# Second-half decay exponentials made between the two halves of kernel generation, and four 64-column products of a transform in a row

## The chip, the cores and the metric

The kernel runs on one core of a Trainium2 chip. The metric is the time of one execution on the device in microseconds (us).

The engines are called as in the profile: PE is the TensorE (PEld its weight loads), DVE the VectorE, ACT the ScalarE, POOL the GpSimd, SP the queue that issues most DMAs.

## The reference, cut to what matters

The reference computes a forward and a backward pass of `x + S4(layernorm(x)) + FFN(layernorm(x))`, length 2048, width 576. The gated FFN has 4608 hidden columns. The S4 layer builds a convolution kernel of length 2048 from 128 modes per channel and applies it by Fourier transforms:

```python
P = jnp.exp(logdA[:, :, None] * l[None, None, :])          # decay exponentials
K = jnp.einsum("dn,dnl,dn->dl", Cc, P, dB).real            # kernel generation
Kf, Uf = rfft2(pad(K)), rfft2(pad(u))
y = irfft2(Uf * Kf)[:L] + u * Dskip
...
_out, _vjp = jax.vjp(_f, ...); return (_out, *_vjp(grad_out))
```

## The kernel before: the parts that matter

Two streams of Python generators are woven into one program. The FFN stream handles 12 chunks of 384 hidden columns. Each chunk starts with the weight gradients of the chunk before (16 to 48 products into one PSUM buffer for each evacuation). Then follow units with a DVE or ACT evacuation after every 3 to 6 products. The S4 stream has these passes: `p1(0)`, `p1(1)` (transform of the inputs, one for each half of the channels), `p2(0)`, `p2(1)` (kernel generation, then `param_grads`), and `p3(0)`, `p3(1)` (transform of the kernel). What a generator yields is its **plan**: microseconds that it takes in the estimate. The weaving uses plan time alone:

```python
PACE = 0.9
W1, W2, W3 = 60.0, 400.0, 58.0
...
    for us in ffn.gen(ln, final):                          # main loop
        ft += us
        ...
        while s4_open and stt < PACE * (ft - start):
            stt += next(sgen)                              # S4 stream (cut)

    def gen(self):                                         # the S4 stream (cut)
        yield from self.both(self.p1(0, 4, 10.0), 68.0, self.params(pw), 45.0)
        ...
        yield from self.both(self.p2(0, pools, pw), 0.8 * W2, self.p1(1, 2, 3.0), W1)
        yield from self.both(self.p2(1, pools, pw), 0.8 * W2, self.p3(0, 2, 3.0), W3)
        yield from self.p3(1, 4, 8.0)
```

A scheduler then orders the instructions of each engine anew; program order is its priority, not the final order. (In the trace of before, the first DVE operation of `p2(1)` starts at 899.99 us, ahead of the last one of `p2(0)`, at 901.46 us.) Each engine then works through its list in order.

The exponentials stand in `params`, two 16-channel groups in each step, for later use through DRAM. The mix is a transform step with 64 output columns for each product; its two outputs take one PSUM buffer each, of three that the S4 stream has:

```python
            def ex_step(i):                                # in params
                shp = [P, 2 * SX, NE]
                ex = exp_.tile(shp, F32, name="exs")       # pool of 3
                v.tensor_tensor(ex[:], pw[...], self.ev[...], op=ALU.mult)
                nc.scalar.activation(ex[:], ex[:], ACT.Exp)
                nc.sync.dma_start(self.ex_dram[:, i:i + 2], ex[...])
            for i in range(0, 8, 2):
                ex_step(i)
                yield 2.0
            ...                                            # other parameters
            for i in range(8, D // SX, 2):
                ex_step(i)
                yield 2.0

    def mix(self, dst, src):
        for o in range(2):
            ps = self.ps()
            for i in range(2):
                nc.tensor.matmul(ps[i * 64:(i + 1) * 64, :DH], lhsT=self.FM[:, o, :], rhs=src[:, i, :], ...)
            g.bal.copy(dst[:, o, :], ps[:, :DH], DH)
            if o == 0:
                yield 0.15
```

Of the kernel before, what the change touches and what calls it, by code (L numbers as in the profile page):

```python
# [2 lines left out]

# [456 lines left out]
class S4:  # L460
# [84 lines left out]
    def params(self, pw):  # L545
        g, nc, bal = self.g, self.g.nc, self.g.bal
        v = nc.vector
        with ExitStack() as c:
            pool = self.pool(c, "par_raw", 1)
            exp_ = self.pool(c, "par_ex", 3)  # L550
            raw = pool.tile([P, 6, D], BF16, name="raw")
            nc.sync.dma_start(raw[:], self.par_in[:])
            ldt = pool.tile([P, D], BF16, name="ldt")
            nc.sync.dma_start(ldt[:], self.log_dt.rearrange("(o d) -> o d", o=1).to_broadcast([P, D]))
            yield 1.0
            dt = pool.tile([P, D], F32, name="dtf")
            nc.scalar.activation(dt[:], ldt[:], ACT.Exp)
            nc.sync.dma_start(self.dt_dram[:], dt[:])
            Ar, Ai, Br, Bi, Cr, Ci = (raw[:, i, :] for i in range(6))
            v.tensor_tensor(pw[:, 0, :], Ar, dt[:], op=ALU.mult)  # L560
            bal.add(d=0.7, a=0.7)
            yield 1.0

            def ex_step(i):
                shp = [P, 2 * SX, NE]
                ex = exp_.tile(shp, F32, name="exs")
                v.tensor_tensor(ex[:], pw[:, 0, i * SX:(i + 2) * SX].unsqueeze(2).to_broadcast(shp), self.ev[:].unsqueeze(1).to_broadcast(shp), op=ALU.mult)
                nc.scalar.activation(ex[:], ex[:], ACT.Exp)
                nc.sync.dma_start(self.ex_dram[:, i:i + 2], ex[:].rearrange("p (i d) e -> p i d e", d=SX))
                bal.add(d=1.4, a=1.2)  # L570

            for i in range(0, 8, 2):
                ex_step(i)
                yield 2.0
            p1 = pool.tile([P, D], F32, name="p1")
            p2 = pool.tile([P, D], F32, name="p2")
            v.scalar_tensor_tensor(pw[:, 1, :], Ai, 1.0 / TWO_PI, dt[:], op0=ALU.mult, op1=ALU.mult)
            for j, (y1, y2, op) in enumerate(((Br, Bi, ALU.subtract), (Bi, Br, ALU.add))):
                v.tensor_tensor(p1[:], Cr, y1, op=ALU.mult)
                v.tensor_tensor(p2[:], Ci, y2, op=ALU.mult)  # L580
                v.tensor_tensor(p1[:], p1[:], p2[:], op=op)
                v.tensor_tensor(pw[:, 2 + j, :], p1[:], dt[:], op=ALU.mult)
                bal.add(d=2.6)
                yield 2.0
            for i in range(8, D // SX, 2):
                ex_step(i)
                yield 2.0

    def dft(self, pool, dram):
        def load(m):  # L590
# [26 lines left out]

    def mix(self, dst, src):
        g, nc = self.g, self.g.nc
        for o in range(2):  # L620
            ps = self.ps()
            for i in range(2):
                nc.tensor.matmul(ps[i * 64:(i + 1) * 64, :DH], lhsT=self.FM[:, o, :], rhs=src[:, i, :], start=True, stop=True)
            g.bal.copy(dst[:, o, :], ps[:, :DH], DH)
            if o == 0:
                yield 0.15

    def unmix(self, dst, src):
        g, nc = self.g, self.g.nc
# [33 lines left out]
    def p1(self, hf, n, gap):  # L663
        g, nc = self.g, self.g.nc
        cols = slice(hf * DH, (hf + 1) * DH)
        with ExitStack() as c:
            ap = self.pool(c, f"p1_a{hf}", n, "right")

            def load(m):
                t = ap.tile([P, 2, 2, DH], BF16, name="sig")  # L670
                nc.sync.dma_start(t[:, 0], g.xn_dram[:, 2 * m:2 * m + 2, cols])
                nc.sync.dma_start(t[:, 1], g.g_v[:, 2 * m:2 * m + 2, cols])
                return lambda i, n2: t[:, i, n2 % 2, :]
            yield from self.fwd1(hf, 2, load, ap, n, gap)
        with ExitStack() as c:
            bp = self.pool(c, f"p1_b{hf}", n, "right")
            fp = self.pool(c, f"p1_f{hf}", 2, "right")
            pp = self.pool(c, f"p1_p{hf}", 1, "right")

            def load_b(h):  # L680
                b = bp.tile([P, 2, 2, DH], BF16, name="b_ug")
                nc.sync.dma_start(b[:], self.mix_in(self.A[2][hf], h))
                return b
            bs = Ahead(load_b, ST, n)
            Z = None
            for h in range(ST + 1):
                old, Z = Z, None
                if h < ST:
                    b = bs.get(h)
                    if h == 0:  # L690
                        yield gap
                    sg = fp.tile([P, 2, 2, DH], BF16, name="s_ug")
                    for i in range(2):
                        yield from self.mix(sg[:, i], b[:, :, i, :])
                        yield 0.15
                    nc.sync.dma_start(self.S[hf][h], sg[:])
                    Z = self.product(fp, pp, sg[:, 1], sg[:, 0], True)
                    yield 0.7
                if old is not None:
                    Ct = fp.tile([P, 2, 1, DH], BF16, name="fC1")  # L700
                    yield from self.unmix(Ct[:, :, 0, :], old)
                    nc.sync.dma_start(self.mix_in(self.C[1][hf], h - 1), Ct[:])
                    yield 0.5
        with ExitStack() as c:
            bp = self.pool(c, f"p1_c{hf}", n + 1, "right")
            dp = self.pool(c, f"p1_d{hf}", 2, "right")

            def load_c(n2):
                Ct = bp.tile([P, 2, 1, DH], BF16, name="bC1")
                nc.sync.dma_start(Ct[:], self.C[1][hf][:, n2])  # L710
                return Ct
            Sx, cs = Ahead(self.dft(bp, self.s3_dram), ST // 2, n), Ahead(load_c, ST, n + 1)
            for n2 in range(ST):
                if n2 % 2 == 0:
                    S3 = Sx.get(n2 // 2)
                Ct = cs.get(n2)
                if n2 == 0:
                    yield gap
                if n2 % 4 == 0:
                    dk = dp.tile([P, DH // SC, 4, SC], BF16, name="dk")  # L720
                g.bal.copy(dk[:, :, n2 % 4, :], self.back2(S3[:, n2 % 2], Ct, 0).rearrange("p (g d) -> p g d", d=SC), DH)
                if n2 % 4 == 3:
                    nc.sync.dma_start(self.dk_dram[hf][:, n2 // 4], dk[:])
                yield 0.5

    def p3(self, hf, n, gap):
# [13 lines left out]
        with ExitStack() as c:  # L740
            bp = self.pool(c, f"p3_b{hf}", n, "right")
            fp = self.pool(c, f"p3_f{hf}", 2, "right")
            zp = self.pool(c, f"p3_z{hf}", 3, "right")
            pp = self.pool(c, f"p3_p{hf}", 1, "right")

            def load_b(h):
                b = bp.tile([P, 2, 1, DH], BF16, name="b_k")
                nc.sync.dma_start(b[:], self.mix_in(self.A[1][hf], h))
                sg = bp.tile([P, 2, 2, DH], BF16, name="s_ug")
                nc.sync.dma_start(sg[:], self.S[hf][h])  # L750
                return b, sg
            bs = Ahead(load_b, ST, n)
            Z = None
            for h in range(ST + 1):
                old, Z = Z, None
                if h < ST:
                    b, sg = bs.get(h)
                    if h == 0:
                        yield gap
                    sk = fp.tile([P, 2, DH], BF16, name="s_k")  # L760
                    yield from self.mix(sk[:], b[:, :, 0, :])
                    Z = self.product(zp, pp, sg[:, 0], sk[:], False), self.product(zp, pp, sg[:, 1], sk[:], True)
                    yield 0.7
                if old is not None:
                    for i in range(2):
                        Ct = fp.tile([P, 2, 1, DH], BF16, name="fC2")
                        yield from self.unmix(Ct[:, :, 0, :], old[i])
                        nc.sync.dma_start(self.mix_in(self.C[2][hf], h - 1)[:, :, i:i + 1, :], Ct[:])
                        yield 0.5
# [207 lines left out]
    def gen(self):  # L977
# [4 lines left out]
        with ExitStack() as cp:  # L982
# [9 lines left out]
            with ExitStack() as c:  # L992
                pools = self.p2_pools(c)
                yield from self.both(self.p2(0, pools, pw), 0.8 * W2, self.p1(1, 2, 3.0), W1)
                yield from self.both(self.p2(1, pools, pw), 0.8 * W2, self.p3(0, 2, 3.0), W3)
            yield from self.p3(1, 4, 8.0)

class Final:
# [201 lines left out]
```

## Time and profile before

| | before |
|---|---|
| time, median of 6 runs | 1849.15 us (1847.29 to 1854.74) |
| PE, DVE, ACT busy | 94%, 75%, 63% |
| exponentials | 18 double steps at 101 to 201 us |
| products of the mix | 384, in 141 groups without a full-width product between them |

The page of the kernel before: busy time, then the span in 40 slices (busy tenths of PE, and the clock that the throttle granted, in tenths).

```profile
PE 1732.4 (94%) x16110; PEld 1180.8 (64%) x16257; DVE 1378.4 (75%) x3223; ACT 1173.4 (63%) x2647; POOL 206.0 (11%) x246
...
PE   7989989999999999999999999999999998899888
...
PEclk9989999999999999999999999999999999999999
```

The windows view of before: stretch, its length, busy us of each engine with the number of instructions, granted clock, DMA share, GB/s.

```profile
96.00:145.00 49.00, 41.22 (x359) 30.55 (x359) 32.61 (x55) 33.26 (x71) 3.05 (x7) 0.86 0.96 332
...
165.00:252.00 87.00, 82.42 (x588) 45.89 (x595) 72.33 (x194) 69.44 (x166) 6.92 (x8) 0.98 0.93 299
...
445.00:740.00 295.00, 287.57 (x2866) 196.00 (x2893) 240.11 (x550) 206.08 (x470) 38.19 (x40) 1.00 0.67 178
795.00:895.00 100.00, 97.74 (x1068) 72.24 (x1072) 75.68 (x163) 71.85 (x161) 18.91 (x20) 1.00 0.74 177
...
1500.00:1616.00 116.00, 98.77 (x666) 55.66 (x674) 84.80 (x265) 77.37 (x210) 6.90 (x8) 1.00 0.88 247
```

PE is the limit through the middle (287.6 of 295 us). It loses time where the first passes (96 to 290 us) and the last (1500 to 1616 us) run.

The timeline of before, where a pair of the mix stands alone (start, duration, engine, line, operation, idle time before it):

```profile
181.14 0.38 PE L235 MATMUL ps_mm<-xT,wd_158 128*128 128x512 bf16 x1 [0.16 <-issue]
181.45 0.31 PE L623 MATMUL ps_s_2640<-b_ug,FM 128*64 128x288 bf16 x2
181.70 0.82 PE L235 MATMUL ps_mm<-xT,wd_158 128*128 128x512 bf16 x3
```

Full-width products follow each other at columns / 2.4 + 2.6 ns in this trace (512 columns 216 ns, 288 columns 122 ns). The 512-column product before the pair therefore takes 0.21 us, but the pair starts 0.31 us later: 0.1 us is the change of array mode. Over all groups, entering takes 96 ns more than columns / 2.4 (median), leaving 98 ns more after four and 123 ns after two. The Trainium skill ("TensorEngine Tiling (Array Packing)", Key Properties) says that changing the tiling mode drains the TensorE; the trace agrees and gives the price.

The exponentials of before (duration min/median/max in ns, first and last start):

```profile
L567 DVE TENSOR_TENSOR exs<-pw,ev x18: 1480/1488/1494, 101.7 to 201.2; 128x1280 f32<-128x1280 f32 x18
L568 ACT ACTIVATE exs<-exs x18: 1269/1274/1357, 103.2 to 207.1; 128x1280 f32<-128x1280 f32 x18
```

### The profile page before, as it was taken

What the parts mean: (1) busy time and instruction counts of PE and PEld (TensorE: products, weight loads), DVE (VectorE), ACT (ScalarE), POOL (GpSimd) and SP (SyncE); (2) the same over time, 40 slices, a digit from 0 to 9 for tenths busy, and PEclk for the clock granted to TensorE, in tenths of its full rate; (3) what the DMA queues carried; (4) which work ended last, traced back from release to release, by engine and by line L of the source; (5) the groups of instructions that cost most, each with busy time, mean ns of one, the idle gap of its engine ahead of it and who ended that gap; (6) DMA issues with size and microseconds to landing.
All of it is one profiled execution on the core that took longest, in us unless ns stands there. A gap on an engine that the chain in (4) does not pass through costs nothing. (4 is left out here: it accounts for less than half of the span.)

```text
span 1848.6 us, 41736 instructions
## 1 busy us (share of the span) xinstructions
PE 1732.4 (94%) x16110; PEld 1180.8 (64%) x16257; DVE 1378.4 (75%) x3223; ACT 1173.4 (63%) x2647; POOL 206.0 (11%) x246
## 2 busy tenths in 40 slices
PE   7989989999999999999999999999999998899888
PEld 5665547667566666766666766766666764476566
DVE  7565975786898787787887889889888658923872
ACT  5865865686587488477477567657747736733432
POOL 0200002112012012002102101202201100010000
PEclk9989999999999999999999999999999999999999
DMA  8798989668557566776676756856754789785763
GB/s 288 263 325 291 332 235 271 197 173 232 177 125 202 182 183 168 212 188 145 195 201 136 234 158 152 235 163 120 188 175 106 174 240 275 207 216 166 253 192 100
DMA packets 236411, 373.26 MB, mean 202 GB/s; under 512 B 49202, under 2 KB 153140, under 8 KB 234676
## 3 DMA queue, kind: packets, MB, share of 16 engines
q1 hardware_dynamic: 210244, 304.08, 50.8%
q0 software_dynamic: 24384, 51.92, 18.5%
q10 hardware_dynamic: 1584, 14.60, 2.3%
q8 instruction: 127, 2.08, 0.5%
q14 instruction: 72, 0.59, 0.1%
HBM read 233.08 MB, written 137.43 MB: 200 GB/s over the span
## 5 line engine op out<-in xcount | busy, mean ns | idle before, releaser
L67 ACT CAST osx<-ps_mm 128x288 bf16<-128x288 f32 x684 | 262.2, 423 | 72.6 <-PE ps_mm L290 60.3
L303 POOL DMA_DIRECT2D acc_dram<-osx x160 | 139.4, 875 | 1036.1 <-ACT osx L67 588.2
L290 PE MATMUL ps_mm<-wf,dgT 128*128 128x288 bf16 x1152 | 208.8, 288 | 17.8 <-ACT osx L67 12.4
L290 PE MATMUL ps_mm<-wf,duT 128*128 128x288 bf16 x1152 | 207.3, 288 | 0.0
L343 PEld LDWEIGHTS <-rows 128*128 128x128 bf16 x1536 | 146.0, 98 | 95.7 <-issue 3.0
L290 PE MATMUL ps_mm<-wf,hT 128*128 128x288 bf16 x1152 | 185.3, 287 | 8.1 <-ACT osx L67 2.3
L235 PE MATMUL ps_mm<-xT,wd_159 128*128 128x512 bf16 x711 | 179.1, 379 | 1.6 <-ACT obw L67 1.1
L235 PE MATMUL ps_mm<-gT,wd_160 128*128 128x512 bf16 x693 | 178.1, 382 | 2.5 <-ACT obw L67 2.0
L235 PE MATMUL ps_mm<-xT,wd_158 128*128 128x512 bf16 x595 | 169.4, 379 | 7.6 <-issue 1.0
L245 DVE SCALAR_TENSOR_TENSOR upm<-rg,ps_mm 128x512 bf16<-128x512 bf16 x144 | 98.2, 682 | 99.6 <-PE ps_mm L235 71.9
L327 PE MATMUL ps_mm<-rows,hN 128*128 128x144 bf16 x2304 | 158.4, 228 | 0.0
L327 PEld LDWEIGHTS <-hN 128*128 128x128 bf16 x2304 | 149.3, 99 | 7.7 <-issue 5.2
L290 PEld LDWEIGHTS <-dgT 128*128 128x128 bf16 x1152 | 109.6, 98 | 53.8 <-issue 25.8
L343 PE MATMUL ps_mm<-duN,rows 128*128 128x384 bf16 x768 | 138.6, 326 | 0.0
L343 PE MATMUL ps_mm<-dgN,rows 128*128 128x384 bf16 x768 | 136.6, 326 | 0.0
L290 PEld LDWEIGHTS <-hT 128*128 128x128 bf16 x1152 | 107.2, 98 | 41.6 <-issue 12.2
L290 PEld LDWEIGHTS <-duT 128*128 128x128 bf16 x1152 | 113.1, 98 | 31.6 <-issue 2.0
L67 ACT CAST obw<-ps_mm 128x384 bf16<-128x384 f32 x105 | 50.1, 477 | 125.2 <-PE ps_mm L343 92.6
L67 ACT CAST dhb<-ps_mm 128x512 bf16<-128x512 f32 x141 | 83.9, 595 | 65.5 <-PE ps_mm L235 63.8
L901 DVE TENSOR_REDUCE Sm<-pr 128x8 f32<-128x256 f32 x288 | 119.2, 414 | 3.6
L243 ACT ACTIVATE rg<-ps_mm 128x512 bf16<-128x512 f32 x144 | 86.9, 604 | 54.8 <-PE ps_mm L235 52.6
L235 PEld LDWEIGHTS <-wd_159 128*128 128x128 bf16 x720 | 65.4, 98 | 62.6 <-issue 2.5
(2513 smaller groups left out, 3512.0 us busy)
## 6 DMA issues: line engine op xcount, KB each, us to landing
acc_dram<-osx POOLq DMA_DIRECT2D x176, 288.0 KB, 4.7
gT<-in_gT_dram SPq DMA_DIRECT2D x48, 640.0 KB, 6.3
xT<-xT_dram SPq DMA_DIRECT2D x44, 640.0 KB, 5.9
rows<-in_gq_dram SPq DMA_DIRECT2D x48, 576.0 KB, 4.7
wf<-in_Wf_dram ACTq DMA_DIRECT2D x11, 1296.0 KB, 9.6
ex_dram<-exs SPq DMA_DIRECT2D x18, 640.0 KB, 6.0
ex<-ex_dram SPq DMA_DIRECT2D x36, 320.0 KB, 3.2
out_dram<-obw SPq DMA_DIRECT2D x96, 96.0 KB, 2.7
```

The costliest lines, as they stand in the source:

```text
L67: self.nc.scalar.copy(out, in_)
L235: nc.tensor.matmul(ps[:], lhsT=w[:, k, fs], rhs=rhs[:, k, :], start=(k == 0), stop=(k == NK - 1))
L243: nc.scalar.activation(rg[:], ps_g[:], ACT.Relu)
L245: nc.vector.scalar_tensor_tensor(upm[:], rg[:], 0.0, ps_u[:], op0=ALU.is_gt, op1=ALU.mult)
L290: nc.tensor.matmul(ps[:, :DH], lhsT=lt, rhs=rh, start=(i == 0), stop=(i == len(mms) - 1))
L303: nc.gpsimd.dma_start(g.acc_dram[:, t, :, :], o[:], accum_op=ALU.add)
L327: nc.tensor.matmul(ps[:, ft * 144:(ft + 1) * 144], lhsT=self.hN[:, st, ft * P:(ft + 1) * P], rhs=gq[:, st, :], start=(st == 0), stop=(st = ...
L343: nc.tensor.matmul(ps[:, :Fc], lhsT=xs[:, st, 0:P], rhs=src[:, st, :], start=(st == 0), stop=(st == ST - 1))
L901: nc.vector.tensor_reduce(out=Sm[:, vi, s0 + dd:s0 + dd + DG, :], in_=pr[:], op=ALU.add, axis=AX.X)
```

## The change

Its intent: take half of the exponentials out of the crowded first stretch and make them just before they are needed, and change the array's mode less often by issuing all four products of a mix together. The pieces also become half as large, and the plan of the third passes grows by 0.15 us a step.

```diff
-            for i in range(0, 8, 2):
-                ex_step(i)
-                yield 2.0
+            for i in range(0, 8):
+                self.ex_step(i, exp_, pw)
+                yield 1.0
 ...
-            for i in range(8, D // SX, 2):
-                ex_step(i)
-                yield 2.0
+            for i in range(8, DH // SX):
+                self.ex_step(i, exp_, pw)
+                yield 1.0
+    def ex_step(self, i, pool, pw):          # one 16-channel group, [P, SX, NE]
+        ...
+    def late_ex(self, pools, pw):
+        for i in range(DH // SX, D // SX):
+            self.ex_step(i, pools[3], pw)    # a pool of 2
+            yield 1.0

     def mix(self, dst, src):
-        for o in range(2):
-            ps = self.ps()
+        pss = [self.ps() for o in range(2)]
+        for o, ps in enumerate(pss):
             for i in range(2):
                 nc.tensor.matmul(...)
+        for o, ps in enumerate(pss):
             g.bal.copy(dst[:, o, :], ps[:, :DH], DH)
-            if o == 0:
-                yield 0.15
 ...                                          # p1: plan 0.15 + 0.15 becomes 0.3
-                    yield from self.mix(sk[:], b[:, :, 0, :])
+                    self.mix(sk[:], b[:, :, 0, :])
+                    yield 0.3                # p3: plan 0.15 becomes 0.3
 ...
-                yield from self.both(self.p2(1, pools, pw), 0.8 * W2, self.p3(0, 2, 3.0), W3)
+                yield from self.both(chain(self.late_ex(pools, pw), self.p2(1, pools, pw)), 0.8 * W2, self.p3(0, 2, 3.0), W3)
```

More of the change, by code (lines that the diff above doesn't have):

```diff
@@ L2 @@
 from contextlib import ExitStack
+from itertools import chain
 import concourse.bass as bass
@@ L562, in params @@
             yield 1.0
-            def ex_step(i):
-                shp = [P, 2 * SX, NE]
-                ex = exp_.tile(shp, F32, name="exs")
-                v.tensor_tensor(ex[:], pw[:, 0, i * SX:(i + 2) * SX].unsqueeze(2).to_broadcast(shp), self.ev[:].unsqueeze(1).to_broadcast(shp), op=ALU.mult)
-                nc.scalar.activation(ex[:], ex[:], ACT.Exp)
-                nc.sync.dma_start(self.ex_dram[:, i:i + 2], ex[:].rearrange("p (i d) e -> p i d e", d=SX))
-                bal.add(d=1.4, a=1.2)
-            for i in range(0, 8, 2):
-                ex_step(i)
-                yield 2.0
+            for i in range(0, 8):
+                self.ex_step(i, exp_, pw)
+                yield 1.0
             p1 = pool.tile([P, D], F32, name="p1")
@@ L584, in params @@
                 yield 2.0
-            for i in range(8, D // SX, 2):
-                ex_step(i)
-                yield 2.0
+            for i in range(8, DH // SX):
+                self.ex_step(i, exp_, pw)
+                yield 1.0
+    def ex_step(self, i, pool, pw):
+        nc = self.g.nc
+        shp = [P, SX, NE]
+        ex = pool.tile(shp, F32, name="ex")
+        nc.vector.tensor_tensor(ex[:], pw[:, 0, i * SX:(i + 1) * SX].unsqueeze(2).to_broadcast(shp), self.ev[:].unsqueeze(1).to_broadcast(shp), op=ALU.mult)
+        nc.scalar.activation(ex[:], ex[:], ACT.Exp)
+        nc.sync.dma_start(self.ex_dram[:, i], ex[:])
+        self.g.bal.add(d=0.75, a=0.65)
+    def late_ex(self, pools, pw):
+        for i in range(DH // SX, D // SX):
+            self.ex_step(i, pools[3], pw)
+            yield 1.0
     def dft(self, pool, dram):
@@ L693, in p1 @@
                     for i in range(2):
-                        yield from self.mix(sg[:, i], b[:, :, i, :])
-                        yield 0.15
+                        self.mix(sg[:, i], b[:, :, i, :])
+                        yield 0.3
                     nc.sync.dma_start(self.S[hf][h], sg[:])
@@ L760, in p3 @@
                     sk = fp.tile([P, 2, DH], BF16, name="s_k")
-                    yield from self.mix(sk[:], b[:, :, 0, :])
+                    self.mix(sk[:], b[:, :, 0, :])
+                    yield 0.3
                     Z = self.product(zp, pp, sg[:, 0], sk[:], False), self.product(zp, pp, sg[:, 1], sk[:], True)
```

## The prediction

> **What bounds the kernel.** One core, 1849 us, mostly bound by the TensorE: the page gives PE 94% busy, DVE 75%, ACT 63%. By stretches (the windows view) PE is 97% busy in 445-740 us and 95% in 1030-1335 us. Weak are the stretches of the first and last transform passes: 96-290 us (PE 41.2 of 49 us at first, granted clock 0.86, DMA share 0.9 and more) and 1500-1616 us (98.8 of 116).
>
> **Part 1: four 64-column products in a row.** The 384 products of the mix have the form 128\*64 and run two at a time. By the starts in the trace they stand in 140 runs (95 of them of two) between full-width products. Entering a run costs 96 ns beyond the streaming time of the product before, leaving it 98 to 123 ns; pairs inside a run follow at about 0.14 us. The list of waits shows it as 32.6 us of "issue" idle before their weight loads. The Trainium skill ("TensorEngine Tiling (Array Packing)", Key Properties) says that a change of tiling mode drains the TensorE; this trace agrees, at about 0.21 us for the way in and out. The edit should leave 80 to 90 runs, some 55 fewer: 11 to 12 us of PE time. In the PE-bound passes (30 of the 55) I count all, in the others half: 9 us. Against it: a mix takes two of three PSUM buffers at once, so some second pairs wait for an evacuation (0.4 us each); I take 1 us off.
>
> **Part 2: exponentials.** 18 double steps at 101-216 us take 18 x 1.49 us of DVE, 18 x 1.27 us of ACT and store 11.8 of the 36.6 MB that the DMA moved there; DVE waited 12.5 us for their stores. PE lost about 9 us there before the first transform's products, waiting for evacuations by ACT and DVE and for issue. Half of this leaves the stretch. I expect 5 us, no more: the loads and the handover between the passes (5 us wait for bC) stay.
>
> They come back at about 900 us as 18 single steps with two buffers. A round is about 0.75 + 0.65 us plus a store of 3 to 5 us: 2.5 to 3 us a step by estimate, some 50 us, where the plan counts 18. The second half of kernel generation starts 20 to 35 us later. DVE is 89% busy there, PE 96%, and PE's own work goes on. ACT has four table loads of 1.28 us, the last (sine) at 232 us; exponentials after it need at least two more. Cost: about 3 us of PE stalls. The last pass (ends 1616 us) has slack: Final's evacuations start at 1700 us.
>
> **Sum.** -8 - 5 + 3 = -10 us. The scheduler orders instructions anew, which alone can move 5 us.
>
> **Predicted: 1839 us, 8 in 10 within 1822 to 1855.** Faster by over 2%: 0.04; within 2%: 0.93; slower by over 2%: 0.03.
>
> **What would show it.** 80-90 runs of 64-column products, mostly of four, cost of entry and exit unchanged; "issue" idle before their weight loads about 20 us. Exponential steps: 18 before 200 us, 18 from about 900 us over 35-60 us, six or more table loads. PE busier in 96-290 us, clock above 0.86. DVE waits for stores of ex at 900-950 us.
>
> **What would make it wrong.** DVE, in order, stuck behind a store at 900 us with FFN products behind it (slower); a late second half pushing the last pass into the final chunk (slower by 10-20 us); the early stretch being limited by exponentials more than I think (faster by 15 us).

## The result

1859.02 us, median of 10 runs (1851.63 to 1862.83), against 1851.14 us for the kernel before in 20 runs (1845.12 to 1854.74). The ratio is 1.0038, 95% interval 1.0025 to 1.0051: slightly slower. Ratios here are the mean time of one kernel's runs over the mean of the other's runs of the same rounds, so not quite the ratio of the medians. The time lies outside the predicted range of 1822 to 1855 us.

The page of the changed kernel, the same rows:

```profile
PE 1733.2 (93%) x16108; PEld 1180.4 (64%) x16257; DVE 1378.9 (74%) x3239; ACT 1182.7 (64%) x2671; POOL 205.6 (11%) x246
...
PE   7989988999999999998999999999999998899888
...
PEclk9999999999999999999999999999999999999999
```

The windows view of the changed kernel, the same stretches:

```profile
96.00:145.00 49.00, 39.88 (x375) 30.70 (x376) 29.48 (x57) 31.04 (x75) 2.86 (x6) 0.93 0.94 327
...
165.00:252.00 87.00, 78.20 (x552) 42.95 (x558) 73.53 (x208) 62.53 (x158) 5.52 (x6) 0.96 0.91 272
...
445.00:740.00 295.00, 284.82 (x2886) 195.64 (x2908) 243.96 (x552) 205.29 (x466) 37.16 (x40) 1.00 0.68 180
795.00:895.00 100.00, 91.09 (x868) 61.38 (x877) 83.73 (x176) 82.04 (x171) 17.81 (x19) 1.00 0.75 197
...
1500.00:1616.00 116.00, 101.98 (x662) 56.57 (x668) 83.28 (x260) 73.87 (x198) 6.90 (x8) 0.97 0.85 241
```

In 795 to 895 us PE falls from 97.7 to 91.1 us busy, while DVE gains 8 and ACT 10 us: there the late exponentials run. In 165 to 252 us, from which work was taken, PE falls too.

The mix in the changed kernel, where it came out as intended: four products as two concurrent pairs, 0.15 us apart.

```profile
511.04 0.14 PEld L630 LDWEIGHTS <-FM 128*64 128x64 bf16 x4
511.04 0.31 PE L630 MATMUL ps_s_8246<-b_ug,FM 128*64 128x288 bf16 x2
511.19 0.29 PE L630 MATMUL ps_s_8247<-b_ug,FM 128*64 128x288 bf16 x2
```

The exponentials of the changed kernel, and the DVE waits in 795 to 895 us:

```profile
L586 DVE TENSOR_TENSOR ex<-pw,ev x36: 810/819/827, 101.6 to 887.8; 128x640 f32<-128x640 f32 x36
L587 ACT ACTIVATE ex<-ex x36: 724/737/811, 102.8 to 889.0; 128x640 f32<-128x640 f32 x36
...
DVE ex L586 <- DMA ex_dram<-ex: 8.4, 4, 4.2
```

The late 18 start at 795 us and end at 888 us: the scheduler pulled them ahead of the end of `p2(0)`.

**Where the time went.** To compare orders that differ everywhere, I worked a number out of each trace. For every weight load, its product should take columns / 2.4 + 2.6 ns (half of that for a product that runs in a pair). What remains of a stretch is time that PE **lost**. (Products of 16 and 32 columns really take 25 ns; that error is the same in all kernels.) The stretches lie between the first weight-gradient products of consecutive FFN chunks, so each holds the same FFN work; the S4 products in it are subtracted too. In before these marks are at 124, 297, 446, 596, 743, 886, 1032, ... 1475, 1645, 1808 us. "Half clock" is the part of the lost time that the clock records explain: length of a stretch at a lowered clock, times what was missing.

| kernel (one traced execution) | lost, 124 to 297 | 743 to 886 | 886 to 1032 | 1475 to 1645 | whole span | of it half clock |
|---|---|---|---|---|---|---|
| before | 35.6 | 7.4 | 13.9 | 33.5 | 225.6 | 18.1 |
| the change | 40.6 | 15.4 | 15.3 | 38.0 | 232.9 | 20.5 |

(Times in the heading are before's marks; each kernel has its own.) The difference of the sums, 7.3 us, is the difference of the spans (1855.9 against 1848.6). The four columns lose 18.9 us more than before: the second FFN chunk, the two chunks around the late exponentials, and the chunk with the last pass. All the rest loses 11.6 us less, of it 4.4 us ahead of the first mark (28.2 in before, 23.8 in the change), and the rest spread over chunks that differ by up to 3 us each. So the net of 7 us is a small difference of larger terms.

### The profile page after: what moved, and what is told of

Read it like the earlier page. It is cut to its first block, busy times and chain, and to the rows that moved or that the text cites. A ratio compares the mean times of both kernels' runs of the same rounds, so it can differ in the third digit from the quotient of the medians.

```text
span 1855.9 us, 41832 instructions
## 1 busy us (share of the span) xinstructions
PE 1733.2 (93%) x16108; PEld 1180.4 (64%) x16257; DVE 1378.9 (74%) x3239; ACT 1182.7 (64%) x2671; POOL 205.6 (11%) x246
## 5 line engine op out<-in xcount | busy, mean ns | idle before, releaser
L291 PEld LDWEIGHTS <-hT 128*128 128x128 bf16 x1152 | 108.1, 99 | 43.4 <-issue 14.5
```

What stands on the lines that cost most here:

```text
L291: nc.tensor.matmul(ps[:, :DH], lhsT=lt, rhs=rh, start=(i == 0), stop=(i == len(mms) - 1))
```

## The experiments

One traced execution carries a few us of chance: e3 and e14 have the same work and plan in the stretch of 124 to 297 us and lose 35.3 and 40.7 us in it. Each run lists its mean granted clock; time x (1 - clock) is what the throttle took at most. Differences of the means over all listed runs (the ratios use the same rounds only, so the two may differ by a us or two):

| run | what it is | ratio to before, 95% interval | difference, us | of it clock | rest |
|---|---|---|---|---|---|
| e1 | mix alone | 0.9997 (0.9982 to 1.0011) | -0.7 | -0.2 | -0.5 |
| e2 | exponentials alone | 1.0024 (1.0005 to 1.0043) | +4.5 | -4.5 | +9.0 |
| e3 | single steps, all early | 0.9977 (0.9961 to 0.9994) | -4.2 | -8.3 | +4.1 |
| e4 | e2 + early slots kept | 1.0101 (1.0075 to 1.0126) | +18.0 | 0.0 | +18.0 |
| e5 | e2 without the late steps | 1.0112 (1.0088 to 1.0136) | +20.0 | +3.1 | +16.9 |
| e6 | e2 without table loads | 1.0039 (1.0010 to 1.0069) | +6.6 | -6.4 | +13.0 |
| e7 | e3 + mix | 1.0001 (0.9974 to 1.0028) | -1.2 | -3.6 | +2.5 |
| e8 | before + 9 empty slots ahead of `p2(1)` | 1.0087 (1.0063 to 1.0110) | +17.0 | +13.8 | +3.2 |
| e9 | before + 18 of them | 1.0058 (1.0043 to 1.0074) | +11.2 | +2.5 | +8.8 |
| e10 | e3 at the plan of e2 | 1.0065 (1.0049 to 1.0081) | +12.4 | -1.8 | +14.3 |
| e11 | late work at before's plan | 1.0048 (1.0026 to 1.0071) | +9.3 | +1.5 | +7.8 |
| e12 | mix, old slots in `p3` | 1.0012 (0.9993 to 1.0031) | +0.8 | -0.2 | +1.0 |
| e13 | before + 9 empty slots ahead of `p3(1)` | 1.0052 (1.0033 to 1.0071) | +9.9 | +8.0 | +1.9 |
| e14 | e3, both waits of `p3(1)` halved, 8 slots in all | 1.0021 (1.0001 to 1.0041) | +4.0 | +0.8 | +3.2 |
| e15 | e3 + e12 + e14 | 0.9983 (0.9967 to 0.9998) | -3.0 | -5.0 | +1.9 |
| e16 | e10, slots ahead of `param_grads` | 1.0078 (1.0058 to 1.0098) | +14.1 | -0.8 | +14.9 |
| e17 | change, late steps ahead of `param_grads` | 1.0076 (1.0058 to 1.0094) | +14.3 | +0.8 | +13.5 |

All 45 runs of before beside them average 1852.9 us, of which the clock took 20.8 us.

The lost time from the traces, as in the table above (us):

| run | 124 to 297 | 743 to 886 | 886 to 1032 | 1475 to 1645 | whole | of it half clock |
|---|---|---|---|---|---|---|
| e1 mix alone | 37.9 | 7.4 | 14.8 | 38.5 | 227.2 | 22.5 |
| e2 exponentials alone | 43.6 | 15.3 | 15.2 | 34.2 | 231.4 | 13.1 |
| e3 single, early | 35.3 | 7.4 | 14.5 | 34.3 | 220.9 | 11.9 |
| e4 e2 + slots | 34.5 | 14.5 | 26.8 | 41.5 | 248.4 | 25.0 |
| e5 no late steps | 39.9 | 13.0 | 19.3 | 40.6 | 246.0 | 15.4 |
| e6 no table loads | 39.1 | 19.0 | 12.8 | 34.2 | 230.1 | 14.1 |
| e7 e3 + mix | 37.0 | 7.5 | 11.3 | 41.8 | 223.9 | 16.4 |
| e8 9 slots | 35.5 | 8.8 | 13.2 | 47.5 | 247.1 | 34.9 |
| e9 18 slots | 35.5 | 7.5 | 15.5 | 45.6 | 236.8 | 24.9 |
| e10 plan of e2 | 51.8 | 13.5 | 13.8 | 33.2 | 237.3 | 17.4 |
| e11 change's place | 34.9 | 14.0 | 22.5 | 34.7 | 237.8 | 25.8 |
| e12 mix, old slots | 36.9 | 7.4 | 10.5 | 34.2 | 221.0 | 17.8 |
| e13 last pass later | 37.3 | 7.4 | 15.7 | 45.0 | 240.5 | 29.4 |
| e14 shorter waits in the last pass | 40.7 | 7.4 | 13.7 | 41.1 | 232.0 | 22.2 |
| e15 e3 + e12 + e14 | 36.8 | 7.5 | 11.9 | 38.8 | 222.1 | 13.0 |
| e16 | 51.3 | 14.8 | 12.2 | 34.3 | 240.2 | 16.5 |
| e17 | 39.0 | 21.1 | 13.4 | 41.4 | 239.5 | 19.8 |

### Which part costs: e1, e2, e3

e1 is before with the mix edit of the diff alone, e2 before with the exponentials' edit alone. e3 is e2 with all steps early:

```diff
-            for i in range(8, DH // SX):
+            for i in range(8, D // SX):          # and no late_ex
                 self.ex_step(i, exp_, pw)
```

> Theory A (the exponentials cost the time, the mix is a small gain): 1846 to 1849 us, 2 to 5 us under the kernel before; runs of 64-column products about 120 instead of 140, 0.2 us each. Theory B (a mix that takes two of three PSUM buffers at once costs the time): 1855 to 1860 us, as the whole change. Theory C (both parts are neutral and only their sum falls badly for the scheduler): within 2 us of before.

> Theory A: 1858 to 1864 us, 8 to 12 us over the kernel before, with the loss of FFN progress near the late exponentials (790 to 890 us) and in 240 to 310 us. Theory B: within 3 us of before. Theory C: within 2 us of before.

> All exponential steps stay early but are 36 single ones, as in the change (mix as before). If it is the smaller size of a step and of its buffers that costs: 1855 us or more. If it is the move to the late place: within 3 us of before, four table loads.

The mix is neutral (0.9997), so theory B, that it costs the time, falls. The exponentials cost (1.0024), theory A by its sign, but 4.5 us and not the 8 to 12 us that it had said. And the smaller pieces are no cost but a gain: 0.9977. Against e3, the move alone costs 0.0047 of 1853 us, or 8.7 us. e3's gain shows in the clock: -8.3 us of it, while the rest is +4.1 us. The windows of before and then of e3 from the start of the exponentials:

```profile
96.00:116.00 20.00, 15.84 (x89) 9.13 (x89) 15.75 (x27) 14.66 (x27) 0.72 (x2) 0.74 0.96 334
116.00:145.00 29.00, 25.39 (x272) 21.41 (x270) 16.86 (x28) 18.59 (x44) 2.32 (x5) 0.94 0.96 330
```

```profile
96.00:116.00 20.00, 17.49 (x122) 11.75 (x122) 17.03 (x34) 15.72 (x36) 1.96 (x4) 0.91 0.93 317
116.00:145.00 29.00, 24.98 (x264) 20.93 (x263) 12.89 (x25) 15.59 (x41) 1.46 (x4) 0.88 1.00 346
```

In the first stretch PE is busy for 17.5 us in place of 15.8, at a clock of 0.91 in place of 0.74; in the second the clock is the lower one in e3 (0.88 against 0.94), so that 1.2 us of the gain are left at 145 us. Ahead of its first mark e3 loses 24.9 us, before 28.2. A likely reason, argued and not isolated, is that a DVE piece of 0.82 us holds up an evacuation behind it for less time than one of 1.49 us.

**Why the mix gains nothing.** The scheduler breaks the four up again: 120 groups in e1 in place of 141, not 85. In the first pass there are 39 against 38 before, and 46 in the whole change. 21 groups fewer at 0.21 us should save about 4.4 us. But the scheduler also put nine full-width products of the last pass into a group of 32 64-column products of the FFN (1527 to 1533 us in e1), which before runs unbroken: ten pieces in place of one, 2.3 us lost in place of 0.1. The change, e7 and e17 show the same. With these counted, PE enters 64-column mode 137 times in e1, 140 in the change and 149 in before. And the waits longer than 0.2 us ahead of the mix's products grow from 2.9 to 6.9 us in the trace. The releaser is the evacuation of the step before (fC), which holds the PSUM buffers. From the view of the mix's weights, what ended the idle time, in before and then in e1:

```profile
  issue: 32.6, 97
...
  ACT fC_19200 L67: 1.0, 1
```

```profile
  issue: 33.6, 96
  ACT fC L67: 4.8, 6
```

So what the fewer groups of the mix save, the broken FFN group and the waits for a second PSUM buffer take. No run separates these two.

### Work or place or plan: e4 to e7

e4 keeps the early plan slots in e2; e5 drops the late steps and with them their 18 us of plan (and reads the first half's exponentials, a wrong result); e6 copies in place of the late exponentials (wrong); e7 is e3 with the mix edit.

```diff
 e4, params:
+            for i in range(DH // SX, D // SX):
+                yield 1.0
 e5:
-chain(self.late_ex(pools, pw), self.p2(1, pools, pw))
+self.p2(1, pools, pw)
-nc.sync.dma_start(ex[:], self.ex_dram[:, hf * (DH // SX) + i])
+nc.sync.dma_start(ex[:], self.ex_dram[:, i])
 e6, late steps only:
-nc.scalar.activation(ex[:], ex[:], ACT.Exp)
+nc.scalar.activation(ex[:], ex[:], ACT.Copy)
```

> Exponentials as in the change (mix as before), but the plan keeps 18 empty slots of 1 us where the moved steps were, so that the first transform pass and the start of kernel generation stand where they stood before. If the loss in the second FFN chunk (43.6 us lost against 35.3) comes from the passes moving forward against the FFN: lost time there back to 34 to 37 us and the whole 6 to 9 us under the exponentials-only kernel, about 1850 us. If it comes from something else in the early steps: no change, about 1858 us.

> Exponentials-only kernel without the 18 late steps; the second half reads the first half's exponentials (wrong result on purpose). If the late steps cost 8 us where they run: the lost time of 747 to 896 us falls from 15 to 7 us and the whole to about 1850 us, while the loss in the second chunk (43 us) stays. If the late steps cost nothing by themselves: about 1858 us.

> Exponentials-only kernel with a copy in place of the late exponentials on ScalarE (wrong result on purpose), so that no table is loaded for them. If the three extra table loads of 1.28 us, and what waits behind them, are the late cost: 4 to 8 us under the exponentials-only kernel, about 1852 us. If it is the work's place on VectorE and its stores: within 2 us of it, about 1857 us.

> All single exponential steps early, and the mix of the change. If the two parts only add up: as the split alone, 0.9975 of before (e1 was 0.9997), 1848 us. If the mix hurts where the passes are crowded: 0.999 or more.

e4: the second chunk was repaired as expected (34.5 us lost), but the whole got slower, 1.0101: the kept slots delay everything after them, and 886 to 1032 us loses 26.8 us. e5 refutes both of my theories of that time at once: with *less* work than e2 the kernel is slower, 1.0112, and 743 to 886 us still loses 13.0 us in place of 7.4. So most of that loss arises there without any late step. But e5 also starts `p2(1)` 18 slots earlier in the plan than e2, so it does not tell what the steps cost by themselves. e6 tests the table loads. In the changed kernel they were:

```profile
794.98 1.28 ACT L587 ACT_TABLE_LOAD   x1
...
799.59 1.28 ACT L821 ACT_TABLE_LOAD   x1
...
815.16 1.28 ACT L587 ACT_TABLE_LOAD   x1
...
891.28 1.28 ACT L821 ACT_TABLE_LOAD   x1
```

Without the loads among the late steps the ratio is 1.0039 against e2's 1.0024, a difference of 0.0015 with an interval of about 0.0035 to each side: no gain is seen, and the expected one of 4 to 8 us is excluded. (The scheduler's PE order differs a little between the two.) e7: the mix on top of e3 gives 1.0001 with a wide interval, so no gain on top of the split is shown; the interval just reaches the sum of the two (0.9974).

### Plan alone, place alone: e8 to e11

New theory: what counts is where the S4 passes stand against the FFN's chunks. e8 and e9 change the plan of before and nothing else; e10 has e3's work at the plan of e2 (the change's without its longer third passes); e11 has e2's work at before's plan.

```diff
 e8, e9 (n = 9, 18):
-self.both(self.p2(1, pools, pw), 0.8 * W2, ...
+self.both(chain([1.0] * n, self.p2(1, pools, pw)), 0.8 * W2, ...
 e10, on e3, with n = 18 as above:
-                yield 1.0
+                yield 1.0 if i < DH // SX else 0.0
 e11, on e4, in late_ex:
-            yield 1.0
+            yield 0.0
```

> The kernel before, with 9 empty slots of 1 us in the plan ahead of the second half of kernel generation: no work is moved or added. Alignment theory (where the second stream meets the chunks of the first decides, by dispersed waits for VectorE and ScalarE): a change of 3 to 15 us, either way. Work theory (only moved work costs): within 2 us of before.

> As the run with 9, with 18 empty slots. Alignment theory: 5 to 20 us slower, as the last pass is pushed back too (the held kernel was 1.0101). Work theory: within 2 us of before.

> All exponentials stay early as single steps, but the plan's time is that of the change: the second half of the steps takes no slots early, and 18 empty slots stand ahead of the second half of kernel generation. Alignment theory: about as the exponentials-only kernel, 1.002 to 1.006 of before, with some 40 us lost in the second chunk. Work theory: as the split alone, 0.998 of before.

> The mirror: the second half of the exponentials is made late, but the plan's time is that of before: 18 empty slots early, and the late steps take no slots. Alignment theory: within 3 us of before or of the split, with the second chunk at 34 to 37 us lost. Work theory: as the exponentials-only kernel, 1.002 to 1.006 of before, with the loss of 747 to 896 us at 15 us.

Nine empty slots, without a single instruction added, cost 0.9%: more than the whole change. Of the 17.0 us, 13.8 are clock, and the trace loses most of it around the last pass, which the slots push back too (47.5 us in place of 33.5). Eighteen slots cost less (e9, 1.0058). e10 shows that the plan of e2 with all work in its old place costs +0.0088 over e3, and e11 that the late place at the old plan costs +0.0071 over e3. Both together (e2) cost only +0.0047. The two effects do not add, so "the cost of the late work" is no fixed number. Of e11 the alignment theory had said "within 3 us of before"; it missed, so the late place has a cost of its own.

### The last pass, the mix's slots, a better kernel: e12 to e15

```diff
 e12, the mix edit, but in p3:
-                    yield 0.3
+                    yield 0.15
 e13:
+            yield from [1.0] * 9
             yield from self.p3(1, 4, 8.0)
 e14, on e3:
-            yield from self.p3(1, 4, 8.0)
+            yield from self.p3(1, 4, 4.0)
 e15: e14 with the mix edit of e12
```

> Kernel before with the mix of four in a row, but 0.15 us a step in the plan of the third passes, as before. If the change's longer slots delayed the last pass and this ate the gain: 0.997 to 0.998 of before, 36 us or less lost in the chunk of 1475 to 1645 us (38.5 with the longer slots, 33.5 before). If waits for PSUM buffers eat it: 0.9997 and 38 us again.

> Kernel before with 9 empty slots ahead of the last pass alone. Alignment theory: the chunk of 1475 to 1645 us loses 43 to 48 us in place of 33.5, all others stay, 1.005 to 1.008 of before. If the last pass has slack, as the prediction said: within 2 us of before.

> The split alone, with the last pass 8 slots earlier in the plan. Alignment theory: the chunk of 1475 to 1645 us loses 26 to 31 us in place of 34.3, 0.993 to 0.996 of before. If only later is worse and its first loads set the time: as the split alone, 0.998.

> Split, mix with the old slots, last pass early. If the three add up: 0.991 to 0.994 of before, 1836 to 1842 us. If their sum is again another alignment: 0.996 or more.

e13 isolates the last pass: 1.0052; its chunk loses 45.0 us in place of 33.5, and 8.0 of the 9.9 us are clock. Its windows show how:

```profile
1548.70:1552.10 3.40, 3.21 (x28) 2.32 (x26) 2.25 (x6) 2.35 (x7) 0.00 (x0) 1.00 0.95 239
1552.10:1555.50 3.40, 0.52 (x5) 0.29 (x3) 0.00 (x0) 0.71 (x2) 0.86 (x1) 1.00 0.70 154
1555.50:1562.30 6.80, 4.63 (x22) 2.29 (x22) 3.56 (x13) 2.10 (x6) 0.00 (x0) 0.50 0.97 300
```

PE is almost idle for 3.4 us, and the clock is 0.50 for the next 6.8 us. The idle stretch is the handover inside the pass: its second part reads from DRAM what the first part stored. The list of PE waits in that chunk has the same wait in before and then in e13:

```profile
PE ps_s_25921 L623 <- DMA b_k<-A_k_186: 1.2, 1, 1.2
```

```profile
PE ps_s L623 <- DMA b_k<-A_k: 5.0, 1, 5.0
```

In before FFN work covers all but 1.2 us of it. In e13 5.0 us stand bare. In e8 it is 7.1 us.

The Trainium skill ("TensorE: Matmul & The Clock Gate", Part 1, What's actually happening) says that the clock goes to half after an idle window of about 3.4 us, and that the windows run free of the kernel. These traces agree: lowered clock is always 0.50 and comes in pieces of 3.4, 6.8 or 10.2 us (13.7 us once each in e4 and e11), apart from the end of the span, and in each trace all changes of the clock stand on one grid of 3.41 us (within 2 ns).

e14 missed (1.0021 against e3's 0.9977; 41.1 us lost in its chunk). But it is no plain shift. The third argument of `p3` is the plan time between the first loads of a part and their use, once at the start and once at the handover. Halving it leaves the first loads where they were and shortens the very wait that e13 laid bare: that wait is 2.5 us here and 2.1 us in e3. Products of the pass's second part also came to stand in the FFN's group of 32 64-column products at 1529 us, which lost 3.7 us in place of 0.1. So it is shown that these shorter waits cost, not that any earlier place is worse. e12 missed too: its trace had the expected 34.2 us in the last pass's chunk, but that execution was the fastest of six (1845.7; the median is 1856.2 us), and the ratio is 1.0012. So the mix gains nothing with either plan. e15 (0.9983) is no better than e3.

### What I could not pin down: e16, e17

743 to 886 us loses 13 us or more in every kernel with the plan of e2 or the late steps. I suspected `param_grads` of the first half, 15 us of DVE work. In before it runs at 884 to 901 us, over the chunk's end at 886, into the weight gradients that need few evacuations. In e10 it runs at 875 to 895 us, ahead of the end at 905.

```diff
 e16, on e10 (and no slots at p2(1)); e17, on the change, with late_ex there:
+        if hf == 0:
+            yield from [1.0] * 18            # e17: yield from self.late_ex(pools, pw)
         yield from self.param_grads(hf, Sm, pw, xp, yop)
```

> As e10 (work early, pace of the change), but the 18 empty slots stand ahead of the first half's parameter gradients in place of behind them. If their place against the chunk is the loss: the chunk before 904 us loses 8 to 9 us in place of 13.5, the second chunk stays at 48 to 52, the whole 4 to 6 us under e10, 1.003 to 1.004 of before. If not: 13 us again and 1.0065.

> The whole change, but the late exponentials stand ahead of the first half's parameter gradients. If the gradients' place is the loss: the chunk before 896 us loses 10 to 12 us in place of 15.4, 1.001 to 1.003 of before. If the late steps are at fault wherever they stand there: 15 us or more, 1.004 or more.

Both missed: 14.8 and 21.1 us lost, 1.0078 and 1.0076. The gradients still began at 876 and 870 us, since the scheduler starts what is ready, whatever the slots say; they only took longer, to 922 and 914 us. So e16 did not test what it should. Which operations cost the stretch ahead of the boundary stays open. It is shown that the plan alone brings 6 us of it (e10, 13.5 against 7.4), with the work in its old place. Two more rows of the table narrow this: the 18 late slots by themselves do nothing there (e9, 7.5), and taking out the early slots without any late ones is enough (e5, 13.0). So the plan's share goes with the early slots that were removed. The late work brings about as much by itself, at before's plan (e11, 14.0).

## Why the prediction was wrong, point by point

- **"some 55 fewer" runs of 64-column products, "9 us", less "1 us".** This step failed. The price of a mode change was right (96 ns in, 98 to 123 ns out). But the number of groups fell from 141 to 122 in the change (120 in e1) and not to 80 to 90, because the scheduler parts the four. PE's entries into 64-column mode fell still less, from 149 to 140 (137 in e1), because a group of the FFN was broken up. And the waits ahead of the mix's products grew by 4 us in e1, not 1. "Issue" idle before their weight loads is 29.9 us in the change, where about 20 was expected. The term of 8 us measured 0.7 us (e1, whose interval includes zero).
- **"I expect 5 us" from taking half the exponentials out of the first stretch.** This step failed too: a gain of that size came without taking them out. e3 leaves all there, in single steps, and gains 4.2 us. I had not counted the smaller piece at all. The change has this gain too (4.4 us less lost ahead of the first mark, 3.3 us in e3), but gives it back: taking the slots out moved the passes forward; the second chunk then lost 40.6 us in the change and 43.6 us in e2, against 35.6 before. PE's busy time in 96 to 290 us, in the four windows that I had read, is 172.5 us before and 172.6 us after.
- **"Cost: about 3 us of PE stalls" late.** Mis-sized: 743 to 1032 us loses 30.7 us in place of 21.3, so 9.4 us. The steps were not at 900 us but at 795 to 888 us, and took 93 us in place of 50. DVE's waits for the stores came as predicted (8.4 us), and the table loads too (eight in all), but the loads are not the main term (e6, no gain without them). The prediction had no term for the plan: taking out the early slots brings a loss of 6 us in 743 to 886 us even with no late step at all (e5, 13.0; e10, 13.5).
- **"The last pass has slack."** Wrong as a step, though it did little in this change: e13 shows that nine slots later cost 9.9 us, eight of them by the clock.
- **"The scheduler orders instructions anew, which alone can move 5 us."** Mis-sized: empty slots alone moved the time by 17 us (e8). My range was drawn around a sum of costs, while the alignment was the larger term.

By time, then: predicted -10 us; measured +7 (0.0038 of 1851 us). Of these 17 us, about 7 are the mix's missing gain (-8 predicted, -0.7 in e1). About 6.5 are the exponentials (-5 + 3 = -2 predicted, +4.5 in e2). Some 3 us are left, within what the parts' intervals allow; whether the two parts also act on each other stays open.

## What to carry to other kernels

In a kernel that weaves two streams by a tuned plan, moved work has no price of its own: measure the plan's shift alone, with empty slots, before explaining a few us by the work. Splitting a long DVE or ACT operation into halves in place was the one gain here (0.9977, a version ahead of both kernels), and a frail one: with further edits on top, e7 and e14 show none. Moving it was a loss. Products written in a row stay in a row only if the scheduler and the PSUM buffers let them: count the groups in the trace.

## What the Trainium skill lacked or had wrong

- "TensorEngine Tiling (Array Packing)", Key Properties: it says that a mode change drains the TensorE but not for how long. Here 96 ns on entering a 64-column group and 98 ns (after four products) to 123 ns (after two) on leaving, beyond streaming time.
- "TensorE: Matmul & The Clock Gate", Part 1: it gives the ramp's penalty as less than 1% of a typical span. That is the warm-up at a start; half-clock windows that recur in mid-kernel took up to 20.8 of 1852.9 us on average in before (1.1%), 33.7 us in e8 (1.8%), and were 8.0 of the 9.9 us of e13. It gives no figure for how busy a window may be and still count as idle; here one with PE busy for 1.93 of 3.4 us (e13, 1576.0 to 1579.4 us) was followed by half clock for 10.2 us. No page says that shifting a program by a few us can add such windows.
- "ScalarE: Activation LUTs", What ACT_TABLE_LOAD costs: about 2.66 us for a switch, 1.28 us for the load and the rest for a drain. In before's trace the load at 232.17 us takes 1.28 us too, but no such drain is seen: it starts 0.02 us after the instruction before it ended (231.75 + 0.40), and the next activation starts at 233.63 us: 1.48 us for the switch, 0.18 us of it a wait for DVE.
